# Decode attention, batch by batch through both layers, with part of K and V kept in SBUF, later tiles loaded by half, and K transposed on VectorE

## The chip, the cores and the metric

The kernel runs on one core of one Trainium2 chip. The metric is the device time of one execution, in microseconds, as a median over repeated runs. A run more than 1.5% above the fastest of its kernel counts as slow; only fast runs are compared. PE is the tensor engine, DVE the vector engine, ACT the scalar engine, POOL is GpSimd, and SP is the engine that issues the transfers.

## The reference

Two identical layers are applied to 8 sequences of one token. Each layer is attention over a cache, and then a small MLP, both behind layer norms. Both layers use the *same* caches and the *same* weights. Only the last 1024 of 4096 cache rows are used.

```python
# B=8 batches, D=640, H=32 heads, Dh=128, W=1024 rows of the cache, F=1728
def A(x, k_cache, v_cache, wq, wo):
    q = (x @ wq) split in 32 heads
    k, v = k_cache[:, :, -1024:], v_cache[:, :, -1024:]
    p = softmax(einsum("bhqd,bhkd->bhqk", q, k) * Dh**-0.5)
    return merge_heads(einsum("bhqk,bhkd->bhqd", p, v)) @ wo
def B(x, w1, b1, w2, b2):
    return gelu(layernorm(x) @ w1 + b1) @ w2 + b2
x = x + A(layernorm(x)); x = x + B(layernorm(x))      # layer 0
x = x + A(layernorm(x)); x = x + B(layernorm(x))      # layer 1
```

One head's K or V of one batch is 1024 x 128 bf16, 256 KB. It is called a *tile* below. There are 8 x 32 x 2 = 512 tiles a layer. The kernel before fetches all of them once for each layer: 1024 tiles, 268 MB, and about 25 MB of weights.

Queries and values are so small that attention hardly moves the result. I computed the reference on a CPU twice (values only, beside the timed runs), once as it is and once with `wo` set to zero, so without attention. The largest output is 0.395, the largest difference 0.00195, and the relative difference (2-norm) 0.19%. The kernel before, run for its values alone, differs from the reference by 0.31%. So attention lies below the kernel's own rounding.

## The kernel before

It goes layer by layer, and within a layer batch by batch. For each head, PE transposes K against an identity (8 matmuls of 128 x 128), and DVE or ACT copies the result out of PSUM. Then the transposed K streams as the moving operand of two N=512 matmuls against a query that is masked to one of 32 output rows. P·V has V as stationary operand and one column of P as the moving one, 8 load+matmul pairs a head.

```python
def transpose_head(self, kn, hi):
    kt_ps = psA.tile([P, NC8, P], BF16, tag="kt_ps")
    for c in range(NC8):
        nc.tensor.transpose(kt_ps[:, c, :], kn[:, hi, c, :], ident_bf[:])   # L143
    if evac_ctr[0] % 5 in (1, 3):
        nc.scalar.copy(ktile[:], kt_ps[:])                                   # L145
    else:
        nc.vector.tensor_copy(ktile[:], kt_ps[:])                            # L147
...
def s_matmuls(s_ps, qz, h, ktile):
    for k in range(2):                       # [32 rows, 512 keys] each         L195
        nc.tensor.matmul(s_ps[...512 columns...], lhsT=qz[:, h, :], rhs=ktile[...])
...
def o_matmuls(b, h, vn, hi, ptg):
    for c in range(NC8):                                                       # L238
        nc.tensor.matmul(ot_ps[:, b, h:h + 1], lhsT=vn[:, hi, c, :], rhs=ptg[:, c, h:h + 1], ...)
...
# loads are 1 MB: four heads of K or of V in one transfer, 5 K buffers and 4 V buffers
nc.sync.dma_start(vn[:], A_v_cache[b, h0:h0 + HB, SK - W:, :].rearrange("h (m c) d -> m h c d", c=NC8))
```

The softmax here doesn't subtract the row's maximum and nothing guards it: scores larger than these inputs give would overflow.

Of the kernel before, what the change touches and what calls it, by code (L numbers as in the profile page):

```python
# [9 lines left out]
BF16 = mybir.dt.bfloat16  # L11
ALU = mybir.AluOpType
ACT = mybir.ActivationFunctionType

P = 128
# [13 lines left out]
HB = 4  # L29
K_BUFS = 5  # L30
V_BUFS = 4
KT_BUFS = 10
NPRE = 8
NPRE0 = 8


def kernel(
    tc, A_x, A_k_cache, A_v_cache, A_wq, A_wo, B_x, B_w1, B_b1, B_w2, B_b2, out
):
    return _kernel(tc, A_x, A_k_cache, A_v_cache, A_wq, A_wo, B_x, B_w1, B_b1, B_w2, B_b2, out)  # L40


@with_exitstack
def _kernel(ctx: ExitStack, tc: tile.TileContext, A_x, A_k_cache, A_v_cache, A_wq, A_wo,
# [7 lines left out]
    wpool = ctx.enter_context(tc.tile_pool(name="wpool", bufs=1, side="right"))  # L52
    state = ctx.enter_context(tc.tile_pool(name="state", bufs=1))
    small = ctx.enter_context(tc.tile_pool(name="small", bufs=2))
    kpool = ctx.enter_context(tc.tile_pool(name="kpool", bufs=K_BUFS))
    vpool = ctx.enter_context(tc.tile_pool(name="vpool", bufs=V_BUFS))
    ktpool = ctx.enter_context(tc.tile_pool(name="ktpool", bufs=KT_BUFS))
    ppool = ctx.enter_context(tc.tile_pool(name="ppool", bufs=2))
    qzpool = ctx.enter_context(tc.tile_pool(name="qzpool", bufs=2))
    psA = ctx.enter_context(tc.tile_pool(name="psA", bufs=3, space=bass.MemoryType.PSUM))  # L60

    ident_bf = const.tile([P, P], BF16)
    make_identity(nc, ident_bf[:])
    eps_t = const.tile([P, 1], FP32)
    nc.vector.memset(eps_t[:], EPS)
    mask32 = const.tile([P, H, H], BF16)
    nc.gpsimd.memset(mask32[:], 0.0)
    nc.gpsimd.affine_select(
        out=mask32[:], in_=mask32[:],
        pattern=[[1, H], [-1, H]],  # L70
        compare_op=ALU.not_equal, fill=1.0, base=0, channel_multiplier=0,
    )

    b1_bf = wpool.tile([P, NFC], BF16)
    nc.vector.memset(b1_bf[:], 0.0)
    with nc.allow_non_contiguous_dma(reason="tiny bias load"):
        nc.gpsimd.dma_start(b1_bf[:, 0:13], B_b1[0:13 * P].rearrange("(fc p) -> p fc", p=P))
        nc.gpsimd.dma_start(b1_bf[0:FLAST, 13:14], B_b1[13 * P:F].rearrange("(fc p) -> p fc", p=FLAST))
    b1_f = wpool.tile([P, NFC], FP32)
    nc.vector.tensor_copy(b1_f[:], b1_bf[:])  # L80
    b2_bf = wpool.tile([NB, D], BF16)
    b2_src = bass.AP(tensor=B_b2.tensor, offset=B_b2.offset, ap=[[0, NB], [1, D]])
    nc.gpsimd.dma_start(b2_bf[:], b2_src)
    b2_f = wpool.tile([NB, D], FP32)
    nc.vector.tensor_copy(b2_f[:], b2_bf[:])
    wq_sb = wpool.tile([P, NKC, H * DH], BF16)
    nc.sync.dma_start(wq_sb[:], A_wq.rearrange("(kc p) n -> p kc n", p=P))

    x_bf0 = state.tile([NB, D], BF16)
    nc.sync.dma_start(x_bf0[:], x_in[:, :])  # L90
    x_f = state.tile([NB, D], FP32)
    nc.vector.tensor_copy(x_f[:], x_bf0[:])
    xn_bf = state.tile([NB, D], BF16)
    xnT = state.tile([P, NKC, NB], BF16)
    qT_bf = state.tile([P, H, NB], BF16)
    ot_bf = state.tile([P, NB, H], BF16)
    y_f = state.tile([NB, D], FP32)
    y_bf = state.tile([NB, D], BF16)
    hT_bf = state.tile([P, NFC, NB], BF16)
    zT = state.tile([P, NKC, NB], BF16)  # L100

    def layernorm(src, dst):
        stats = small.tile([NB, 2, 6], FP32, tag="ln_stats")
        nc.vector.bn_stats(stats[:, 0, :], src[:, 0:D // 2])
        nc.vector.bn_stats(stats[:, 1, :], src[:, D // 2:D])
        mv = small.tile([NB, 2], FP32, tag="ln_mv")
        nc.vector.bn_aggr(mv[:], stats[:])  # L107
        rstd = small.tile([NB, 1], FP32, tag="ln_rstd")
        nc.scalar.activation(rstd[:], mv[:, 1:2], ACT.Sqrt, bias=eps_t[:NB, :], scale=1.0)  # L109
        nc.vector.reciprocal(rstd[:], rstd[:])  # L110
        nc.vector.tensor_scalar(out=dst, in0=src, scalar1=mv[:, 0:1], scalar2=rstd[:, 0:1],
                                op0=ALU.subtract, op1=ALU.mult)

    def make_T(ps_pool, src_bf, dst_T):
        pt = ps_pool.tile([P, NKC, NB], BF16, tag="xT_ps")
        for kc in range(NKC):
            nc.tensor.transpose(pt[:, kc, :], src_bf[:, kc * P:(kc + 1) * P], ident_bf[:NB, :NB])
        nc.vector.tensor_copy(dst_T[:], pt[:])

    evac_ctr = [0]  # L120

    class AttnLayer:
        def __init__(self, idx):
            self.idx = idx
            self.pre_kt = {}
            self.k_tiles = {}

        def load_k(self, b, h0, prefetch_only=False):
            key = (b, h0)
            if key in self.k_tiles:  # L130
                return self.k_tiles[key] if prefetch_only else self.k_tiles.pop(key)
            kn = kpool.tile([P, HB, NC8, DH], BF16, tag="kn")
            src = A_k_cache[b, h0:h0 + HB, SK - W:, :].rearrange("h (m c) d -> m h c d", c=NC8)
            nc.sync.dma_start(kn[:], src)
            if prefetch_only:
                self.k_tiles[key] = kn
            return kn

        def transpose_head(self, kn, hi):
            ktile = ktpool.tile([P, NC8, P], BF16, tag="kt")  # L140
            kt_ps = psA.tile([P, NC8, P], BF16, tag="kt_ps")
            for c in range(NC8):
                nc.tensor.transpose(kt_ps[:, c, :], kn[:, hi, c, :], ident_bf[:])  # L143
            if evac_ctr[0] % 5 in (1, 3):
                nc.scalar.copy(ktile[:], kt_ps[:])  # L145
            else:
                nc.vector.tensor_copy(ktile[:], kt_ps[:])  # L147
            evac_ctr[0] += 1
            return ktile

        def prologue_step(self, b, h):
            kn = self.load_k(b, (h // HB) * HB, prefetch_only=True)
            self.pre_kt[(b, h)] = self.transpose_head(kn, h % HB)

        def run(self, mctx, transition_fn=None, pre_q_fn=None, post_o_fn=None):
            li = self.idx

            for h0 in range(0, H, HB)[:5]:
                self.load_k(0, h0, prefetch_only=True)

            if pre_q_fn is not None:
                pre_q_fn()

            with tc.tile_pool(name=f"psq{li}", bufs=1, space=bass.MemoryType.PSUM) as psq:
                layernorm(x_f, xn_bf)
                make_T(psq, xn_bf, xnT)
                qT_ps = psq.tile([P, H, NB], FP32, tag="qT_ps")
                for h in range(H):
                    for kc in range(NKC):
                        nc.tensor.matmul(qT_ps[:, h, :], lhsT=wq_sb[:, kc, h * DH:(h + 1) * DH],  # L170
                                         rhs=xnT[:, kc, :], start=(kc == 0), stop=(kc == NKC - 1))
                nc.vector.tensor_copy(qT_bf[:], qT_ps[:])

            wctx = ExitStack()
            wopool = wctx.enter_context(tc.tile_pool(name=f"wopool{li}", bufs=1, side="right"))
            wo_sb = wopool.tile([P, H, D], BF16, tag="wo")
            nc.sync.dma_start(wo_sb[:], A_wo.rearrange("(h p) n -> p h n", p=P))

            def build_qz(b):
                qz = qzpool.tile([P, H, H], BF16, tag="qz")  # L180
                nc.vector.tensor_tensor(out=qz[:], in0=qT_bf[:, :, b:b + 1].to_broadcast([P, H, H]),  # L181
                                        in1=mask32[:], op=ALU.mult)
                return qz

            with ExitStack() as ictx:
                psS = ictx.enter_context(tc.tile_pool(name=f"psS{li}", bufs=2, space=bass.MemoryType.PSUM))
                psO = ictx.enter_context(tc.tile_pool(name=f"psO{li}", bufs=1, space=bass.MemoryType.PSUM))

                def alloc_s():
                    s_ps = psS.tile([H, NC8, P], FP32, tag="s_ps")  # L190
                    return s_ps

                def s_matmuls(s_ps, qz, h, ktile):
                    for k in range(2):
                        nc.tensor.matmul(s_ps[:, 4 * k:4 * k + 4, :].rearrange("p c m -> p (c m)"),  # L195
                                         lhsT=qz[:, h, :],
                                         rhs=ktile[:, 4 * k:4 * k + 4, :].rearrange("p c m -> p (c m)"),
# [207 lines left out]
```

## Time and profile before

The median is 821.6 us over 6 runs (819.9 to 823.9).

| what | number | where it is read |
|---|---|---|
| traffic | 293 MB, 357 GB/s on average | queue table |
| plateau of the transfers | about 385 GB/s | slices |
| PE busy | 86% | engines |
| chain of waits | 79% PE | chain |
| SP waiting for P·V to free V buffers | 433 us | waits of the DMA queue |

The page's parts for engines, slices (40 slices of the span, DMA in tenths of busy time, GB/s moved), queues and chain:

```profile
span 821.3 us, 21636 instructions
PE 702.5 (86%) x10008; PEld 487.9 (59%) x10008; DVE 263.8 (32%) x449; ACT 236.3 (29%) x285; POOL 7.2 (1%) x15
...
DMA  9999999999999999999899899999999999999814
GB/s 334 375 382 386 386 385 386 386 385 386 383 382 376 386 383 379 382 379 380 311 349 328 320 385 380 369 386 376 382 384 380 386 374 386 377 387 334 300 65 159
...
q1 hardware_dynamic: 148912, 293.05, 97.8%
...
PE 79%; DMA 9%; ACT 6%; DVE 3%; issue 2%; SPq 0%; ACTq 0%; DVEq 0%
```

The costliest groups (line, engine, operation, out<-in with shapes and count | busy us, mean ns of one | idle before, releaser):

```profile
L147 DVE COPY ktile<-kt_ps 128x1024 bf16<-128x1024 bf16 x307 | 205.9, 689 | 397.4 <-PE kt_ps L143 394.5
L145 ACT COPY ktile<-kt_ps 128x1024 bf16<-128x1024 bf16 x205 | 203.9, 1012 | 444.2 <-PE kt_ps L143 434.7
L143 PE MATMUL kt_ps<-ident_bf,kn 128*128 128x128 bf16 x4096 | 288.4, 231 | 33.0 <-DMA kn<-in_A_k_cache_dram 22.8
...
L195 PE MATMUL s_ps<-ktile,qz 128*32 128x512 bf16 x1024 | 272.4, 395 | 1.8 <-DVE qz L181 1.8
...
L238 PE MATMUL po_tile<-ptg,vn 128*128 128x1 bf16 x4096 | 122.3, 164 | 18.1 <-DMA vn<-in_A_v_cache_dram 12.8
```

PE's transposes and scores are 561 of its 702 busy us. At the same time the 16 DMA engines are busy for 97.8% of the span, so the two bounds stand beside each other. The waits of the DMA queue (waiter <- awaited: us in total, times, longest) say that transfers start when P·V frees a buffer:

```profile
SPq L231 <- PE po_tile L238: 433.0, 110, 7.9
```

One line of PE's timeline (start, length, engine, line, operation) is the yardstick for the change's many small matmuls. It shows 160 pairs of weight load and N=8 matmul in 4.41 us, 27.5 ns a pair:

```profile
427.05 4.41 PE L170 MATMUL qT_ps<-xnT,wq_sb 128*128 128x8 bf16 x160 [0.27 <-DVE xnT L118]
```

### The profile page before, as it was taken

How to read it: one execution, taken by the hardware profiler on the slowest of the kernel's cores; microseconds unless marked ns; L12 is line 12 of the kernel's file. 1: busy time of each engine (PE TensorE's matmuls, PEld its weight loads, DVE VectorE, ACT ScalarE, POOL GpSimd, SP SyncE). 2: the span in 40 equal slices, each digit the busy share in tenths (PEclk: the TensorE clock that was granted, in tenths of full speed). 3: DMA queues.
4: the chain of work that ended last, by engine and by line, in shares of the span. 5: the costliest groups of instructions: out<-in, count | busy, mean ns of one | idle time of the engine just before them, and what ended most of it. 6: DMA issues, size and time to landing. Idle time of an engine off the chain costs nothing.

```text
span 821.3 us, 21636 instructions
## 1 busy us (share of the span) xinstructions
PE 702.5 (86%) x10008; PEld 487.9 (59%) x10008; DVE 263.8 (32%) x449; ACT 236.3 (29%) x285; POOL 7.2 (1%) x15
## 2 busy tenths in 40 slices
PE   0889989898989899996759998989898989989463
PEld 0756656566666666666435666666666656666432
DVE  1433332334333332331224433333323333323122
ACT  0234323323233323233003423332232333232200
POOL 2000000000000000000000000000000000000000
PEclk9899989898989989897858998989899998989676
DMA  9999999999999999999899899999999999999814
GB/s 334 375 382 386 386 385 386 386 385 386 383 382 376 386 383 379 382 379 380 311 349 328 320 385 380 369 386 376 382 384 380 386 374 386 377 387 334 300 65 159
DMA packets 149114, 294.44 MB, mean 359 GB/s; under 512 B 4360, under 2 KB 16032, under 8 KB 148384
## 3 DMA queue, kind: packets, MB, share of 16 engines
q1 hardware_dynamic: 148912, 293.05, 97.8%
q8 instruction: 78, 1.28, 0.6%
q0 software_dynamic: 112, 0.01, 0.1%
q14 instruction: 12, 0.10, 0.0%
HBM read 293.04 MB, written 0.01 MB: 357 GB/s over the span
## 4 chain that ended last, share of the span: by engine, by line
PE 79%; DMA 9%; ACT 6%; DVE 3%; issue 2%; SPq 0%; ACTq 0%; DVEq 0%
PE s_ps L195 31%; PE kt_ps L143 29%; PE po_tile L238 13%; ACT ktile L145 4%; DMA kn<-in_A_k_cache_dram 4%; DMA w_sb<-in_B_w_dram 3%; DMA vn<-in_A_v_cache_dram 2%; PE att_ps L301 2%; PE o_ps L347 1%; ACT pe L203 1%; PE qT_ps L170 1%; ACT pe L206 1%; DVE pe L212 1%; PE po_tile L214 1%; PE att_ps L303 1%
## 5 line engine op out<-in xcount | busy, mean ns | idle before, releaser
L147 DVE COPY ktile<-kt_ps 128x1024 bf16<-128x1024 bf16 x307 | 205.9, 689 | 397.4 <-PE kt_ps L143 394.5
L145 ACT COPY ktile<-kt_ps 128x1024 bf16<-128x1024 bf16 x205 | 203.9, 1012 | 444.2 <-PE kt_ps L143 434.7
L143 PE MATMUL kt_ps<-ident_bf,kn 128*128 128x128 bf16 x4096 | 288.4, 231 | 33.0 <-DMA kn<-in_A_k_cache_dram 22.8
L143 PEld LDWEIGHTS <-kn 128*128 128x128 bf16 x4096 | 258.3, 104 | 87.1 <-issue 63.1
L195 PE MATMUL s_ps<-ktile,qz 128*32 128x512 bf16 x1024 | 272.4, 395 | 1.8 <-DVE qz L181 1.8
L238 PEld LDWEIGHTS <-vn 128*128 128x128 bf16 x4096 | 113.4, 97 | 60.4 <-issue 46.6
L195 PEld LDWEIGHTS <-qz 128*32 128x32 bf16 x1024 | 83.8, 98 | 95.0 <-issue 15.7
L238 PE MATMUL po_tile<-ptg,vn 128*128 128x1 bf16 x4096 | 122.3, 164 | 18.1 <-DMA vn<-in_A_v_cache_dram 12.8
L214 PE MATMUL po_tile<-ident_bf,pe 32*128 32x32 bf16 x128 | 5.9, 179 | 32.3 <-DVE pe L212 32.3
L181 DVE TENSOR_TENSOR qz<-qT_bf,mask 128x1024 bf16<-128x1024 bf16 x16 | 19.5, 1224 | 29.9 <-PE s_ps L195 29.7
L214 PEld LDWEIGHTS <-pe 32*128 32x128 bf16 x128 | 4.6, 97 | 39.0 <-ACT pe L206 38.8
L109 ACT ACTIVATE rstd<-mv,eps_t 8x1 f32<-8x1 f32 x6 | 1.8, 293 | 82.8 <-DVE mv L107 82.8
L301 PE MATMUL att_ps<-wo_sb,ot_bf 128*8 128x512 bf16 x64 | 21.7, 441 | 1.0 <-DVE ot_bf L295 1.0
L347 PE MATMUL o_ps<-w_sb,hT_bf 128*8 128x512 bf16 x28 | 11.9, 519 | 9.4 <-DMA w_sb<-in_B_w_dram 9.4
L203 ACT ACTIVATE pe<-s_ps 32x512 bf16<-32x512 f32 x16 | 9.4, 586 | 33.5 <-PE s_ps L195 33.5
L303 PE MATMUL att_ps<-wo_sb,ot_bf 128*8 128x128 bf16 x64 | 15.4, 241 | 0.0
L301 PEld LDWEIGHTS <-ot_bf 128*8 128x8 bf16 x64 | 6.5, 101 | 11.6 <-issue 4.8
L170 PE MATMUL qT_ps<-xnT,wq_sb 128*128 128x8 bf16 x320 | 8.8, 167 | 2.4 <-issue 2.2
L170 PEld LDWEIGHTS <-wq_sb 128*128 128x128 bf16 x320 | 8.7, 101 | 2.5 <-issue 2.5
L206 ACT ACTIVATE pe<-s_ps 32x512 bf16<-32x512 f32 x16 | 9.1, 569 | 0.0
L347 PEld LDWEIGHTS <-hT_bf 128*8 128x8 bf16 x28 | 3.1, 109 | 10.1 <-issue 4.7
L295 DVE CAST ot_bf<-po_tile 128x256 bf16<-128x256 f32 x2 | 0.8, 425 | 24.9 <-PE po_tile L238 24.9
(59 smaller groups left out, 91.0 us busy)
## 6 DMA issues: line engine op xcount, KB each, us to landing
kn<-in_A_k_cache_dram SPq DMA_DIRECT2D x128, 1024.0 KB, 12.2
vn<-in_A_v_cache_dram SPq DMA_DIRECT2D x128, 1024.0 KB, 9.5
wo_sb<-in_A_wo_dram SPq DMA_DIRECT2D x2, 5120.0 KB, 23.1
wq_sb<-in_A_wq_dram SPq DMA_DIRECT2D x1, 5120.0 KB, 16.4
w_sb<-in_B_w_dram SPq DMA_DIRECT2D x2, 2160.0 KB, 7.9
w_sb<-in_B_w_dram SPq DMA_DIRECT2D x2, 2080.0 KB, 14.8
w_sb<-in_B_w_dram SPq DMA_DIRECT2D x2, 80.0 KB, 13.5
x_bf<-in_A_x_dram SPq DMA_DIRECT2D x1, 10.0 KB
```

Of the source, the lines that this page charges most:

```text
L143: nc.tensor.transpose(kt_ps[:, c, :], kn[:, hi, c, :], ident_bf[:])
L145: nc.scalar.copy(ktile[:], kt_ps[:])
L147: nc.vector.tensor_copy(ktile[:], kt_ps[:])
L170: nc.tensor.matmul(qT_ps[:, h, :], lhsT=wq_sb[:, kc, h * DH:(h + 1) * DH], rhs=xnT[:, kc, :], start=(kc == 0), stop=(kc == NKC - 1))
L181: nc.vector.tensor_tensor(out=qz[:], in0=qT_bf[:, :, b:b + 1].to_broadcast([P, H, H]), in1=mask32[:], op=ALU.mult)
L195: nc.tensor.matmul(s_ps[:, 4 * k:4 * k + 4, :].rearrange("p c m -> p (c m)"), lhsT=qz[:, h, :], rhs=ktile[:, 4 * k:4 * k + 4, :].rearrange ...
L203: nc.scalar.activation(pe[:, 0:4, :].rearrange("p c m -> p (c m)"), s_ps[:, 0:4, :].rearrange("p c m -> p (c m)"), ACT.Exp, scale=QSCALE, ...
L214: nc.tensor.transpose(pt_ps[:, c, :], pe[:, c, :], ident_bf[:H, :H])
L238: nc.tensor.matmul(ot_ps[:, b, h:h + 1], lhsT=vn[:, hi, c, :], rhs=ptg[:, c, h:h + 1], start=(c == 0), stop=(c == NC8 - 1))
L301: nc.tensor.matmul(att_ps[:, 0:512], lhsT=lhsT, rhs=wo_sb[:, h, 0:512], start=(h == 0), stop=(h == H - 1))
L303: nc.tensor.matmul(att_ps[:, 512:D], lhsT=lhsT, rhs=wo_sb[:, h, 512:D], start=(h == 0), stop=(h == H - 1))
L347: nc.tensor.matmul(o2_ps[:, 0:512], lhsT=hT_bf[:, fc, :], rhs=w2_sb[:, fc, 0:512], start=(fc == 0), stop=(fc == NFC - 1))
```

## The change

Its intent is to fetch less and to take the K transposes and the wide score matmuls off PE.

1. It is batch-major. Batch b runs through layer 0, its MLP and its queries of layer 1. After layer 0, 14 of its 32 heads keep K and V in SBUF (28 of 41 tile slots), so that layer 1 needs no second fetch of them. The other 18 heads are streamed again. Batch b-1's streamed heads run interleaved with batch b's MLP. Weights are loaded once.
2. DVE transposes K in SBUF, one instruction a tile, as 32-bit words. The code reckons with 32 x 32 blocks, each transposed for itself. So each group of 32 partitions holds *other* keys, and the query is spread into 4 columns, each masked to one group. K becomes the stationary operand (128 keys, stride of two bf16), with 4 moving columns: 8 pairs a head.
3. Heads go in groups of up to 8. Per group: scores, one exp, 16 small PE matmuls that turn P, a copy out of PSUM on DVE, row sums by a matmul with ones, P·V.
4. Loads are one tile each instead of four, from a pool of slots in first-in-first-out order.

The core of the diff (cut):

```diff
-        def transpose_head(self, kn, hi):
-            for c in range(NC8):
-                nc.tensor.transpose(kt_ps[:, c, :], kn[:, hi, c, :], ident_bf[:])
-            ...copy kt_ps -> ktile on DVE or ACT...
+    def load(job, which, h):
+        s = take()
+        n = DH * NC8 // 2 if s in filled else DH * NC8
+        filled.add(s)
+        nc.sync.dma_start(slots[s][:, 0:n],
+                          cache[job.b, h, SK - W:, :].rearrange("(m c) d -> m (c d)", c=NC8)[:, 0:n])
+    def s_head(job, hi):
+        ...
+            nc.vector.transpose(slots[kt] as uint32 "p (j gt c) -> p j gt c",
+                                slots[kn] as uint32 "p (gt j r) -> p j gt r")
+        for g in range(2):
+            for j in range(2):
+                for e in range(2):
+                    o = 512 * j + 256 * g + e
+                    nc.tensor.matmul(job.s_ps[:, hi, g, :], lhsT=k[:, o:o + 255:2],
+                                     rhs=qd[:, h, 2 * j + e, :], ...)
+    def softmax(job):
+        nc.scalar.activation(p_s[:, 0:n], job.s_ps[:, 0:n], ACT.Exp, scale=QSCALE)
+        ...16 matmuls p_s -> p_ps...
+        nc.vector.tensor_copy(job.p_v[:, :, 0:n, :], p_ps[...])
+        ...8 matmuls with ones -> sums...
+    def finish(job):
+        nc.vector.reciprocal(rd[:, 0:n], job.o_ps[:, 1, 0:n])
+        nc.vector.tensor_tensor(out=dst, in0=job.o_ps[:, 0, 0:n], in1=rd[:, 0:n], op=ALU.mult)
+    for b in range(NB):
+        drain(run_jobs(jobs))                          # layer 0 of b, 5 groups
+        ch = chain(b)                                  # MLP and layer-1 query of b
+        merge(run_jobs(again), ch, 1)                  # with layer 1, streamed heads of b-1
+        drain(run_jobs(keep(b, 1)))                    # layer 1, kept heads of b
```

**The line with `n` is not an optimisation that keeps the function.** A slot that has been filled once receives only the first half of its next tile. The other half keeps what lay there before. Nearly all loads (759 of 800) are such halves, so about half of the keys and values that enter attention belong to another head or batch.

## The prediction

> **What bounds the kernel now.** Two things. The page's slices show the DMA engines busy nearly throughout, at about 385 GB/s (queue table: 293 MB, 97.8% of 16 engines' span). The chain of waits is 79% PE: scores 31%, K transposes 29%, P·V 13%. SP spends 433 us waiting for P·V to free V buffers (the DMA queue's waits). Relieving one side alone would gain little.
>
> **What the change does.**
> 1. Traffic. Batch by batch, 14 of 32 heads keep K and V in SBUF between the layers, and weights are loaded once. Cache tiles (256 KB) fetched fall from 1024 to 800. And, unannounced: a slot that was filled once gets only half of its next tile; the other half is stale. About 45 loads are full, 755 are 128 KB. I count 110 MB of cache plus 15 MB of weights: 125 MB, 325 us at 385 GB/s. This is no longer the reference's attention; I expect it to pass only because attention's contribution is tiny here.
> 2. PE. 4096 K transposes (288 us busy) and 1024 N=512 score matmuls (272 us) go. K tiles become stationary, with 4 moving columns: 4096 load+matmul pairs, beside 4096 for P·V as before. Added: about 1920 pairs for softmax, 1280 projection, 2400 per-batch MLP and q. Total about 14,300. The timeline shows 160 such pairs (q, N=8) in 4.41 us at a granted clock of 0.50: 27.5 ns a pair. So PE about 395 us.
> 3. DVE takes the K transposes: 400 instructions of 512 32-bit elements. [...] this trace has no DVE transpose, but its f32 operations fit that (256 elements: 425 ns, 112: 274). Estimate 0.66 to 0.70 us each, 270 us, plus about 80 us of small operations. ACT's 204 us of PSUM copies go.
> 4. DMA issue: 800 loads of one tile instead of 256 of four. An issue on SP's timeline takes 0.37 to 0.51 us: about 330 us.
>
> No engine exceeds 400 us, so dependencies set the time. DVE is in order: the P copy out of PSUM stands before the next group's transposes, so each group of up to 8 heads costs its transposes plus one round of scores, exp, PE transpose and copy; from such hops in the present chain I estimate 1.6 us a group.
>
> **Sum (estimates).** Layer 0 of a batch: 32 x 0.66 + 5 x 1.6 + 3 = 32 us. Layer 1's streamed heads, with MLP and q woven in: 24. Kept heads, PE bound: 10. That is 66 x 8 = 528. The first batch waits for full tiles and all weights (29 MB, 85 us instead of 32): +53. Last stream and tail +38, minus 4 where batch 0 has no stream: about 615; some waits should overlap, so 600 us. All of the gain is on the critical path, since both old bounds fall.
>
> **Signs.** DMA traffic near 125 MB, around 200 GB/s; transposes 0.65 to 0.75 us, x400; PE pairs near 27 ns; DVE idle mostly ended by PE around the softmax copy; a chain mixed between DVE, PE and ACT; a DMA-bound first 85 us.
>
> **What would make it wrong.** Weights read with a stride of two elements may load slower (54 ns a pair would add 110 us to PE). A DVE transpose at half that rate adds 270 us. Too few small loads may be in flight while 28 of 41 slots are kept. If groups overlap better than I think, 500 us. Results could fail the tolerance; the time would stand.
>
> Predicted 600 us, 510 to 690; faster 0.96, same 0.02, slower 0.02.

A straight line through two f32 operations (425 ns for 256 elements, 274 ns for 112) gives 0.69 us for 512 elements, an estimate within the range that was put. The sum came to 615 us, with 0.66 us a transpose, and was rounded to 600 us. That DVE keeps the program's order, and that a stride of two costs no time, is checked below on the trace of the changed kernel (a wait of 1.15 us; 0.21 us a step for both strides).

## The result

The changed kernel takes 637.1 us (635.7 to 638.9, 8 runs), against 822.2 us for the kernel before in 16 runs. The ratio is 0.775 (0.774 to 0.777). Ratios here are the mean time of one kernel's fast runs over that of the other's of the same rounds, so not quite the ratio of the medians that are quoted.

The page after, the same parts:

```profile
span 636.8 us, 31626 instructions
PE 454.4 (71%) x14400; PEld 425.1 (67%) x14400; DVE 325.9 (51%) x855; ACT 20.7 (3%) x99; POOL 13.8 (2%) x27
...
DMA  7999960866768666865677476766677577847620
GB/s 289 388 375 356 310 192 11 234 194 174 200 186 230 171 197 184 237 181 157 181 216 223 138 205 187 226 171 179 175 209 206 160 211 205 234 132 197 188 80 2
...
q1 hardware_dynamic: 122534, 125.22, 66.1%
```

Traffic is 125 MB as counted. After the first five slices the transfers run at about half of their plateau. No engine is busy for more than 71%. The page's chain of waits breaks off in this trace (a stretch of 42 us is given as "issue"), so it isn't used. The groups that replace the five above:

```profile
L239 DVE STREAM_TRANSPOSE slot<-slot 128x512 uint32<-128x512 uint32 x400 | 250.7, 680 | 19.2 <-DMA slot<-in_A_k_cache_dram 14.7
L249 PE MATMUL s_ps<-qd,slot 128*128 128x4 bf16 x4096 | 180.6, 168 | 77.5 <-DVE slot L239 55.2
...
L277 PE MATMUL o_ps<-p_v,slot 128*128 128x1 bf16 x4096 | 169.1, 165 | 19.7 <-DMA slot<-in_A_v_cache_dram 18.4
...
L288 DVE RECIPROCAL rd<-o_ps 128x8 f32<-128x8 f32 (+2 forms) x80 | 15.3, 192 | 115.0 <-PE o_ps L277 114.2
...
L266 DVE CAST p_v<-p_ps 128x64 bf16<-128x64 f32 (+2 forms) x80 | 16.7, 208 | 50.1 <-PE p_ps L262 49.9
```

Scores now wait for DVE's transposes (55 us), and DVE waits 114 us for P·V before it may form a group's result (`finish`, L288) and 50 us before it copies P (L266). SP's waits for P·V have shrunk from 433 us:

```profile
SPq L228 <- PE o_ps L277: 91.0, 102, 19.4
SPq L228 <- DVE slot L239: 62.7, 109, 4.0
```

DVE's timeline of layer 0 of one batch shows the rhythm:

```profile
322.13 4.86 DVE L239 STREAM_TRANSPOSE slot<-slot 128x512 uint32<-128x512 uint32 x8
328.14 0.23 DVE L266 CAST p_v<-p_ps 128x64 bf16<-128x64 f32 x1 [1.15 <-PE p_ps L262]
328.28 4.85 DVE L239 STREAM_TRANSPOSE slot<-slot 128x512 uint32<-128x512 uint32 x8
...
334.28 0.22 DVE L266 CAST p_v<-p_ps 128x64 bf16<-128x64 f32 x1 [0.66 <-PE p_ps L262]
334.43 1.29 DVE L239 STREAM_TRANSPOSE slot<-slot 128x512 uint32<-128x512 uint32 x2
338.26 0.21 DVE L288 RECIPROCAL rd<-o_ps 128x8 f32<-128x8 f32 x1 [2.54 <-PE o_ps L277]
...
338.64 0.17 DVE L266 CAST p_v<-p_ps 128x16 bf16<-128x16 f32 x1
338.73 4.85 DVE L239 STREAM_TRANSPOSE slot<-slot 128x512 uint32<-128x512 uint32 x8
```

Eight transposes take 4.85 us, 0.61 us each. From the end of a group's transposes to the start of the next group's, DVE loses 1.3 us (326.99 to 328.28) where the group has 8 heads, and 3.0 us (335.72 to 338.73) behind the group of 2, where PE still has eight heads of P·V and projection to do. DVE keeps the program's order here: the copy waits 1.15 us for PE, and the eight transposes that the program has behind it start only after the copy has, at 328.28. With the copy on ACT and `finish` later, ten transposes run across such a group's end without a pause (act_copy_defer below, 6.04 us).

The three stages of one batch in the steady state, by windows of the trace (busy us and instructions of each engine, granted clock, DMA share, GB/s): the streamed heads of the batch before with this batch's MLP and query (from DVE's addition of attention to x up to the first score of a kept head); the kept heads (up to the first transpose of the next batch); layer 0 of the next batch.

```profile
285.85:313.21 27.36, 20.91 (x673) 20.19 (x674) 15.35 (x46) 0.82 (x5) 1.08 (x2) 1.00 0.62 173
313.21:322.13 8.92, 7.45 (x278) 7.32 (x274) 1.33 (x9) 0.43 (x2) 0.00 (x0) 1.00 0.51 158
322.13:355.62 33.49, 25.98 (x796) 23.57 (x796) 23.04 (x50) 1.06 (x5) 0.00 (x0) 1.00 0.75 215
```

The columns in parentheses belong to PE, PE's weight loads, DVE, ACT and POOL in this order. In no stage is any engine, or the DMA, busy all the time.

A mark in the trace tells batches apart: DVE adds each batch's attention to its x once. These marks stand at 88.3, 147.5, then on average every 69.6 us up to 565.4 us, and the rest takes 71.4 us. The six middle batches are the *steady period* below, each between two marks.

### The profile page after: what moved, and what is told of

Same layout as the page of the kernel before. It is cut to its first block, busy times and chain, and to the rows that moved or that the text cites. A ratio compares the mean times of both kernels' runs of the same rounds, so it can differ in the third digit from the quotient of the medians.

```text
span 636.8 us, 31626 instructions
## 1 busy us (share of the span) xinstructions
PE 454.4 (71%) x14400; PEld 425.1 (67%) x14400; DVE 325.9 (51%) x855; ACT 20.7 (3%) x99; POOL 13.8 (2%) x27
## 3 DMA queue, kind: packets, MB, share of 16 engines
q1 hardware_dynamic: 122534, 125.22, 66.1%
## 5 line engine op out<-in xcount | busy, mean ns | idle before, releaser
L239 DVE STREAM_TRANSPOSE slot<-slot 128x512 uint32<-128x512 uint32 x400 | 250.7, 680 | 19.2 <-DMA slot<-in_A_k_cache_dram 14.7
L249 PE MATMUL s_ps<-qd,slot 128*128 128x4 bf16 x4096 | 180.6, 168 | 77.5 <-DVE slot L239 55.2
L249 PEld LDWEIGHTS <-slot 128*128 128x128 bf16 x4096 | 146.4, 105 | 103.2 <-DVE slot L239 71.9
L277 PE MATMUL o_ps<-p_v,slot 128*128 128x1 bf16 x4096 | 169.1, 165 | 19.7 <-DMA slot<-in_A_v_cache_dram 18.4
L277 PEld LDWEIGHTS <-slot 128*128 128x128 bf16 x4096 | 144.2, 104 | 21.2 <-DMA slot<-in_A_v_cache_dram 19.6
L288 DVE RECIPROCAL rd<-o_ps 128x8 f32<-128x8 f32 (+2 forms) x80 | 15.3, 192 | 115.0 <-PE o_ps L277 114.2
L305 PE MATMUL att<-ot,wo_sb 128*128 128x1 bf16 x1280 | 62.1, 165 | 2.4 <-issue 1.8
L305 PEld LDWEIGHTS <-wo_sb 128*128 128x128 bf16 x1280 | 49.8, 104 | 2.8 <-issue 1.8
L270 PE MATMUL o_ps<-p_v,ones_bf 128*128 128x8 bf16 (+2 forms) x640 | 28.3, 167 | 29.2 <-DVE p_v L266 29.2
L270 PEld LDWEIGHTS <-ones_bf 128*128 128x128 bf16 x640 | 29.5, 104 | 28.7 <-issue 26.7
L266 DVE CAST p_v<-p_ps 128x64 bf16<-128x64 f32 (+2 forms) x80 | 16.7, 208 | 50.1 <-PE p_ps L262 49.9
L388 PE MATMUL q_ps<-xn,wq_sb 128*128 128x1 bf16 x1280 | 38.5, 165 | 2.1 <-DVE xn L166 1.7
L183 PEld LDWEIGHTS <-w_sb 128*128 128x128 bf16 x630 | 18.6, 104 | 4.7 <-DVE yT L171 2.9
L205 PEld LDWEIGHTS <-w_sb 128*128 128x128 bf16 x630 | 18.6, 104 | 3.5 <-DVE g L199 2.0
```

Source lines behind the costliest of these rows:

```text
L183: nc.tensor.matmul(h_ps[:, fc, :], lhsT=w1_sb[:, kc, fc * P:(fc + 1) * P], rhs=yT[:, kc, :], start=(kc == 0), stop=(kc == NKC - 1))
L205: nc.tensor.matmul(o_ps[:, n, :], lhsT=w2_sb[:, fc, n * P:(n + 1) * P], rhs=g2[:, fc, :], start=(fc == 0), stop=(fc == NFC - 1))
L239: nc.vector.transpose(slots[kt][:].bitcast(U32).rearrange("p (j gt c) -> p j gt c", j=2, c=32), slots[kn][:].bitcast(U32).rearrange("p (gt ...
L249: nc.tensor.matmul(job.s_ps[:, hi, g, :], lhsT=k[:, o:o + 255:2], rhs=qd[:, h, 2 * j + e, :], start=(j == 0 and e == 0), stop=(j == 1 and ...
L266: nc.vector.tensor_copy(job.p_v[:, :, 0:n, :], p_ps[:, :, 0:2 * n].rearrange("p t (h g) -> p t h g", g=2))
L270: nc.tensor.matmul(job.o_ps[:, 1, 0:n], lhsT=ones_bf[:], rhs=job.p_v[:, c % 4, 0:n, c // 4], start=(c == 0), stop=(c == NC8 - 1))
```

## The experiments

All twelve kernels of the experiments were accepted as correct, which says little about attention, as will be seen. The first four ran on one chip and the next two sets of four on others, each set with its own runs of the kernel before (822.9, 820.9 and 825.7 us).

| kernel | loads | us | ratio to before | first mark, us | steady period, us |
|---|---|---|---|---|---|
| changed | halves, 14 kept | 637.1 | 0.775 | 88.3 | 69.6 |
| full_loads | whole, 14 kept | 697.8 | 0.848 | 92.0 | 77.1 |
| nokeep_half | halves, 0 kept | 671.1 | 0.816 | 89.3 | 73.7 |
| nokeep_full | whole, 0 kept | 778.3 | 0.947 | 92.5 | 87.4 |
| no_reload | once per slot | 616.1 | 0.749 | 72.3 | 68.6 |
| act_copy | halves, 14 kept | 625.6 | 0.761 | 88.3 | 68.3 |
| act_copy_defer | halves, 14 kept | 622.9 | 0.758 | 88.7 | 67.8 |
| skew | halves, 14 kept | 626.3 | 0.762 | 89.6 | 68.4 |
| skew_full | whole, 14 kept | 701.3 | 0.855 | 92.0 | 77.8 |
| skew_no_reload | once per slot | 599.9 | 0.728 | 76.6 | 66.1 |
| skew_keep8 | halves, 8 kept | 628.0 | 0.762 | 88.6 | 68.0 |
| fused | halves, 14 kept | 625.3 (3 fast runs) | 0.757 | not used | not used |
| fused_full | whole, 14 kept | 702.0 | 0.852 | 92.4 | 77.7 |

### Where the gain comes from: undoing the halves and the keeping

**full_loads** loads every tile whole, and so computes the reference:

```diff
-        n = DH * NC8 // 2 if s in filled else DH * NC8
+        n = DH * NC8
```

> Every cache tile loaded whole, so this one computes the reference's attention. Cache 800 x 256 KB = 210 MB, with weights about 225 MB. Theory A (in the changed kernel the DMA is off the critical path by a small margin, DVE/PE dependencies set its 69 us a batch): 26.2 MB a batch is 68 us at 385 GB/s against 69 us, and the 9.7 us with only kept heads have few free slots to fill, so some of it comes out on top: 680 to 720 us, DMA busy over 90%. Rival B (halved loads are a main source of the gain and the whole kernel is still paced by its data): about 637 x 225/125, over 800 us, no gain left over the kernel before.

Measured: 697.8 us (695.9 to 698.7), inside theory A's range. The queue table and the transposes' group of this run:

```profile
q1 hardware_dynamic: 122534, 224.70, 91.0%
...
L239 DVE STREAM_TRANSPOSE slot<-slot 128x512 uint32<-128x512 uint32 x400 | 254.8, 684 | 39.8 <-DMA slot<-in_A_k_cache_dram 35.8
```

With whole tiles the DMA is again nearly the bound (91% busy), and DVE's transposes wait 36 us for K instead of 15 us. So with 14 heads kept the halving is worth 61 us of the 185 us, and the function-keeping rest of the change gains 15%.

**nokeep_half** sets `NKEEP = 0` and leaves the halves in.

> NKEEP = 0, half loads left in. 112 more K tiles are loaded and transposed (DVE +68 us busy, DMA +29 MB). Theory A (time is the sum of stages whose length DVE's order and PE set; kept heads only shift the K transposes out of a PE-bound stage of 9.7 us): the kept stage vanishes and the streamed layer-1 stage grows by 14 x 0.6 us + one group: 625 to 655 us, about the same as with kept heads. Rival B (keeping heads is what gained, by traffic or by transposes): 637 + 40 to 70 us.

Measured: 671.1 us (668.1 to 674.6), between the two: keeping heads is worth 34 us here, not the 0 to 18 us of A nor the 40 to 70 us of B. DVE has 512 transposes instead of 400, and they wait 42 us for K instead of 15 us, so both DVE and the supply of K have less room. Theory A had put the whole effect down to the order of stages and is too simple.

**nokeep_full** does both.

> NKEEP = 0 and full loads: 1024 full tiles, 283 MB, so nearly the kernel before's traffic with the new PE and DVE work. Theory A: DMA bound, 283 MB at 385 GB/s = 735 us, measured 740 to 775 us; so the new way of computing alone, at equal cache traffic, gains 50 to 80 us by filling the DMA's gaps. Rival B (the way of computing gains nothing without less data): 810 to 830 us.

Measured: 778.3 us (776.7 to 783.5), just above theory A's range. The queue table:

```profile
q1 hardware_dynamic: 154790, 283.44, 100.0%
```

At nearly the traffic of the kernel before (283 against 293 MB), the new way of computing gains 44 us and leaves the DMA busy for the whole span. The gain then can only be what a steadier stream and 10 MB fewer weights (an estimate of 25 us at 385 GB/s) give. Batch-major order, transposes on DVE and small loads weren't undone one by one, so their shares of the 44 us stay open.

The parts one after the other, whole tiles first: 822 → 778 (new computing) → 698 (14 heads kept, 59 MB less) → 637 us (halves, 99 MB less). At the plateau of 385 GB/s these two cuts are 152 us and 258 us of transfer time. They brought 81 and 61 us. The difference is where the transfers ceased to be the bound. With the halves first the same end is reached by 778 → 671 → 637 us: then the halves bring 107 us and the kept heads 34 us. So neither part has a share of its own; what each is worth depends on whether the other is there.

**no_reload** fills each slot once and never again:

```diff
-        n = DH * NC8 // 2 if s in filled else DH * NC8
+        if s not in filled:
+            nc.sync.dma_start(...the whole tile...)
         filled.add(s)
-        nc.sync.dma_start(...n columns...)
```

> Wrong on purpose: a slot is loaded once and never again, later heads read whatever lies there. Only about 26 MB move after which the DMA is idle. Theory A (half loads are off the critical path after the first batch): only the first batch gets shorter, by 6 to 10 us: 620 to 632 us. Rival B (loads, or SP issuing 800 of them, still pace the steady state): below 600 us. On the result: if the comparison with the reference passes here too, the tolerance can not see attention, and passing says nothing about the half loads.

Measured: 616.1 us (615.9 to 616.6), a little below A's range and far from B's. Of the 21 us, 16 us lie before the first mark (88.3 to 72.3 us), where the first batch waits for whole tiles and weights. A steady period falls from 69.6 to 68.6 us. So in the changed kernel the transfers cost 1 us a batch once it is under way: theory A, though the first batch gained more than the 6 to 10 us that I had expected. And a kernel whose attention runs almost wholly on stale data passes. The comparison with the reference can't see attention with these inputs.

To see the fault of the halves itself I ran three programs for their values on a CPU, with both caches multiplied by 400, which makes attention up to 0.38 of an output of at most 0.63. The relative errors (2-norm) against the reference with the same inputs are 0.0056 for the kernel before, 0.0056 for full_loads and 0.585 for the changed kernel. These runs give values only, no times.

### What sets the steady period: DVE's order, PE's order, or the tiles

The prediction said that DVE's order makes each group cost one softmax round on top of its transposes. Three kernels take parts of that round away step by step.

**act_copy** lets ACT copy P:

```diff
-        nc.vector.tensor_copy(job.p_v[:, :, 0:n, :], p_ps[...])
+        nc.scalar.copy(job.p_v[:, :, 0:n, :], p_ps[...])
```

> The changed kernel with the copy of P out of PSUM moved from DVE to ACT (half loads left in). Theory A (DVE's order is what each group pays: its transposes of the next group stand behind this copy, 1.3 us from the last transpose of a group to the first of the next in the trace): DVE passes the softmax, but still waits in finish for the last P.V of the group before; about 0.5 us on each of 64 transposing groups saved: 600 to 618 us. Rival B (PE's own stream sets the pace: it waits for exp and copy whichever engine copies): 632 to 642 us.

Measured: 625.6 us (622.2 to 628.6). That is neither A's 600 to 618 nor B's 632 to 642.

**act_copy_defer** also calls `finish` two heads into the next group:

```diff
             for hi in range(GH):
+                if hi == 2 and fin is not None:
+                    finish(fin); old, fin = (fin if fin.layer == 0 else None), None
                 ...
-            if prev is not None:
-                finish(prev)
+            old, fin = None, prev
```

> As the last, and finish (reciprocal and product on DVE) put two heads later, behind the first two transposes of the next group, so that DVE has nothing to wait for between groups. Theory A: transposes run on through the softmax, 585 to 612 us, the pause between groups gone from DVE's timeline. Rival B: 630 to 642 us.

Measured: 622.9 us (619.9 to 626.1), again between the two. Theory A's sign did come: the pause between two groups of 8 is gone where nothing else holds DVE. This is DVE's timeline of layer 0 of one batch:

```profile
318.60 6.04 DVE L239 STREAM_TRANSPOSE slot<-slot 128x512 uint32<-128x512 uint32 x10
325.75 4.87 DVE L239 STREAM_TRANSPOSE slot<-slot 128x512 uint32<-128x512 uint32 x8 [1.10 <-PE s_ps L249]
...
330.82 0.70 DVE L239 STREAM_TRANSPOSE slot<-slot 128x512 uint32<-128x512 uint32 x1
331.71 0.71 DVE L239 STREAM_TRANSPOSE slot<-slot 128x512 uint32<-128x512 uint32 x1 [0.19 <-PE s_ps L249]
334.35 0.21 DVE L288 RECIPROCAL rd<-o_ps 128x8 f32<-128x8 f32 x1 [1.93 <-PE o_ps L277]
```

Ten transposes now run in one go across the group's end. But then DVE stands still for 1.1 us because a slot to write to is still being read by scores on PE, and for 1.9 us because P·V is not done. The wait wasn't removed but moved. The sum shows it too: in the changed kernel DVE waits 50 us in all before the copy of P, and 14 us came, while the wait before `finish` grew from 114 to 138 us.

**skew** changes PE's order as well, so that PE has scores of the next group to do while ACT forms exp and copies P:

```diff
+                    s_head(job, hi)
+                    if hi == len(job.heads) - 1:
+                        sm_exp(job)                  # exp right after the group's last score
+                if prev is not None and hi == 0:
+                    sm_turn(prev)                    # PE turns P one head into the next group
+                if prev is not None and hi == LAG - 1:
+                    sm_sum(prev)                     # LAG = 2
+                ...o_head(prev, hi - LAG), finish and projection later still...
```

> As the last, and PE's order changed too: a group's exp is issued right after its last score, and its PE transpose, sums and P.V come one and two heads into the next group, so that PE has scores to do meanwhile. If both engines pay for the softmax round (theory C: DVE's stall and PE's stall of 0.35 us at two places of each of 80 groups are hidden in each other, and only removing both shows): 555 to 590 us, and the difference to the last is 20 us or more. If DVE alone paid (A): within 10 us of the last.

Measured: 626.3 us (623.9 to 628.0), no better than the last. Theory C's number falls: freeing PE of the softmax round, too, brings nothing. But this order also puts P·V later, and `finish` still stands on DVE, before transposes:

```profile
L295 DVE RECIPROCAL rd<-o_ps 128x8 f32<-128x8 f32 (+2 forms) x80 | 15.5, 194 | 161.4 <-PE o_ps L284 161.4
```

The copy's 50 us of waiting are gone from DVE, and the wait before `finish` is 47 us longer than in the changed kernel: 161 us for both then (50 + 114 = 164 us in the changed kernel), in both kernels partly where DVE has nothing else to do. So no run had a DVE that doesn't wait for PE between groups, and theory C was not tested in full.

**skew_no_reload** asks whether the supply of tiles had taken the stall's place: it is skew with the edit of no_reload.

> Wrong on purpose: the reordered kernel (P copied by ACT, finish late, PE skewed) with slots loaded once and never again, as in the run that only took the loads away (616 us). Theory D (the two waits stand in parallel: with the softmax stall removed the steady state falls back on the supply of tiles, as loads wait for one of the 13 slots that the kept heads leave, which ate the gain): taking both away gives much more than the sum of the two single gains (21 us and 11 us): 560 to 590 us. Rival E (after the stall something else on PE or DVE, not supply, keeps the 69 us a batch): 600 to 612 us, about the sum of the single gains.

Measured: 599.9 us (599.3 to 600.4), at the lower edge of E's range. Rival E stands and theory D falls: taking away the transfers (21 us) and the stalls (11 us) brings 37 us together, only 5 us above the sum. The same three stages as above, in this run:

```profile
265.83:292.77 26.94, 20.76 (x678) 19.88 (x679) 15.03 (x43) 1.63 (x8) 1.08 (x2) 1.00 0.01 3
292.77:301.37 8.60, 7.64 (x273) 7.26 (x269) 1.11 (x7) 0.84 (x4) 0.00 (x0) 1.00 0.01 4
301.37:332.88 31.51, 25.30 (x796) 22.73 (x796) 22.00 (x46) 2.07 (x10) 0.00 (x0) 1.00 0.02 4
```

With no reloads to wait for and no copy of P in DVE's order, layer 0 is 31.5 us instead of 33.5 us, and the first stage has hardly moved (26.9 against 27.4 us). PE is busy for 54 us of 67 us, DVE for 38 us. So taking the round's copy and the transfers away together is worth 3.5 us of a period of 69.6 us. The other 66 us lie elsewhere. That is not the worth of all of DVE's waits for PE: within layer 0 its pauses between transposes fell only from 6.9 to 4.4 us, since `finish` waits for P·V before the transposes that follow it, once for 2.5 us. There the chain of waits of this run goes through `finish`, from P·V to the transposes of the next group (start, length, what):

```profile
316.98 0.23 PE o_ps L284 x8
317.23 0.22 DVE rd L295
317.48 0.17 DVE ot L301
317.64 4.77 DVE slot L240 x8
```

No run took `finish` off DVE.

Where the other 66 us lie is argued, not shown. It is probably PE's stream of small pairs, and the fill and drain of three stages in turn: 14,400 pairs over the whole kernel, at the 26.7 ns a pair of PE's timeline, are 384 us, and of PE's idle time within a period (13 us of 67 us here) 9 us are scores that wait for DVE's transposes (53.3 us in six periods). No run took pairs away from PE, so how much they bind stays open. It is also open how much a PE that waits less in one place loses in the next because DVE's transposes are then late; the waits of scores for transposes rose from 55 to 85 us between the changed kernel and skew:

```profile
PE s_ps L250 <- DVE slot L240: 84.8, 144, 8.0
```

The chain of waits of skew_no_reload, which covers nearly all of its span, shows the same mixture, with shares of the span by engine:

```profile
PE 50%; DVE 22%; issue 13%; DMA 10%; POOL 2%; SPq 1%; ACT 1%; POOLq 0%; ACTq 0%
```

### For speed: other splits, and the versions that compute the reference

**skew_keep8** keeps 8 heads, so that 12 more slots are free for the stream.

> The reordered kernel with half loads and 8 kept heads instead of 14: 12 more slots for the stream, 48 more K tiles to load and transpose (DVE +30 us busy, DMA +12.6 MB). Theory D: the slots gained are worth more than the transposes cost: 595 to 618 us. Rival E: slower than with 14 kept, 630 to 645 us, as without kept heads in the original order (671 for 0 kept).

Measured: 628.0 us (627.0 to 630.0), the same as with 14 within the runs' scatter (626.3). It falls between the ranges of D and E: the added transposes and transfers and the freed slots seem to cancel (argued from the total alone). Between 8 and 14 the time is flat; with 0 kept the original order lost 34 us.

**fused** puts the kept heads' groups into one run of groups with the next batch's layer 0:

```diff
-            jobs = nxt + kept
+            jobs = keep(b - 1, 1) + nxt + kept
-        drain(run_jobs(keep(b, 1)))
```

> The reordered kernel with half loads, 14 kept heads, and the kept heads' second-layer groups put into the same run of groups as the next batch's first layer, so that DVE can transpose while PE works on kept heads and their slots come free during the stream. Theory D: slots come free no earlier in PE's order, but one pipeline drain a batch is saved, 2 to 3 us each: 600 to 615 us. Rival E: the same 2 to 3 us, so this run is for speed, not for telling apart.

Measured: 625.3 us in the three fast runs (620.3 to 626.6), outside the expected 600 to 615. The fourth, the profiled one, was slow (630.8 us), so its trace is not used. The saving of a drain (2 to 3 us a batch, the estimate) is not to be seen.

**skew_full** and **fused_full** are skew and fused with whole tiles, the candidates for a fast kernel that computes the reference.

> The last with full loads, so that it computes the reference's attention. 225 MB at 385 GB/s are 584 us; the first batch and the tail have about 25 us with little DMA. With the compute side relieved, DMA should be the bound: 640 to 675 us, DMA busy over 92%, against 698 us with full loads alone.

> The same with full loads, computing the reference's attention. The DMA is nearly the bound (91% busy in 698 us with full loads alone), so only its gaps can be won: 670 to 695 us.

Measured: 701.3 us (698.3 to 705.4) and 702.0 us (699.0 to 704.5). Both missed their ranges; neither is faster than full_loads alone (697.8 us). The waits of skew_full say where the freed time went:

```profile
DVE slot L240 <- DMA slot<-in_A_k_cache_dram: 87.8, 86, 7.8
```

DVE waits 88 us for K tiles, against 36 us in full_loads, with the DMA 90.5% busy. With whole tiles the transfers are the bound, and a better order of computing only waits longer for them.

So no run beat the changed kernel while computing the reference. The kernel to use of those measured is full_loads: 15% faster than before, and right.

## Why the prediction was right or wrong

The time was 637 us against 600 us predicted, within 510 to 690 us, and the gain was clear. Point by point:

- **Traffic, 125 MB: right** (125.2 MB), with the halves seen beforehand. That the result would pass because attention is tiny was right, and no_reload and the CPU values show it.
- **PE, 14,300 pairs of 27.5 ns: right.** There are 14,400. PE's timeline where scores and P·V alternate, in steps of 8 pairs:

```profile
316.48 0.35 PE L249 MATMUL s_ps<-qd,slot 128*128 128x4 bf16 x8
316.69 0.35 PE L277 MATMUL o_ps<-p_v,slot 128*128 128x1 bf16 x8
...
318.19 0.35 PE L249 MATMUL s_ps<-qd,slot 128*128 128x4 bf16 x8
```

  The starts of the first and the last line are 64 pairs and 1.71 us apart, 26.7 ns a pair. The 0.35 us of a step is longer than the 0.21 us to the next because one matmul's record lasts 165 ns (L277's mean): seven starts of 26.7 ns and one record are 0.35 us. The fear of slow loads with a stride of two was unfounded. One load's record is 104 ns here, but loads overlap and a pair starts every 26.7 ns. Stride 2 (scores) is no slower than stride 1 (P·V): 0.21 us a row of eight for both.
- **Transposes, 0.66 to 0.70 us: right for one, slightly high for a row of them.** One is 0.68 us in the profile, and eight take 4.85 us, 0.61 us each.
- **No engine exceeds 400 us: wrong for PE**, whose busy time is 454 us, since every short row of pairs ends with a record of 165 ns that is counted as busy in full. It didn't matter for the sum, which was built from pairs.
- **The sum, 615 us: nearly right, stage by stage.** The first mark was put at 85 us and came at 88.3. Batch 0's second part (66 - 4 = 62 us) took 59.2. Six periods of 66 us took 69.6 each. The end (24 + 10 + 38 = 72 us) took 71.4. So the miss is 3.6 us in each of six periods, 22 us. It sits in two terms: the stage of streamed heads with MLP and query (24 us, measured 27.4; the kept heads, 10 us, took 8.9) and layer 0 (32 us, measured 33.5, with a drain of 7 us behind the last transposes where 3 us and one round, 4.6 us, were put, and 3.0 us behind the group of two).
- **"Some waits should overlap, so 600 us": wrong.** This step had no number behind it. The measured time lies above the sum, not below it, and the step made the prediction worse by 15 us.
- **"The P copy stands before the next group's transposes, so each group costs its transposes plus one round, 1.6 us": right as a description, overstated as a cost.** The pause is there (1.3 us). But taking the copy out of DVE's order brought 11 to 14 us of the 50 us that DVE waits before it, and the wait before `finish` grew by 24 to 47 us in the same runs. The sign "DVE idle mostly ended by PE around the softmax copy" had it too: DVE's larger wait was the 114 us before `finish`, for P·V, which the prediction doesn't name. A stall that comes back at the engine's next need of PE was counted as if it were the price. What the waits before `finish` cost in all is not shown.
- **All of the gain is on the critical path since both bounds fall: right in direction**, but the bounds didn't fall equally. With the transfers at 283 MB, only 44 us came, and each further cut of the traffic brought less than its transfer time.
- **First 85 us bound by the DMA: right.** no_reload shortened it by 16 us, and it is the only place where the changed kernel's transfers cost much.

## What to carry to other kernels

Undo a large change one part at a time before its gain is explained, and check first that each part keeps the function: here the last third of the gain (61 of 185 us, with the other parts in place) came from loads that leave half of each tile stale, and a comparison in which attention is below rounding couldn't see it. A pause on one engine's timeline is not worth its length (here, of 50 us of waits before the copy 11 to 14 us were won): before it is removed, look for the next thing that the engine needs from the other, since the wait can come back there. In a sum of stages, leave out rounding for "overlap" that has no number.

## Costs measured here

- A DVE transpose of 128 x 512 uint32 takes 680 ns (the mean of 400 in the changed kernel), and 0.61 us each in a row of eight. Viewed as bf16 that is 128 x 1024.
- A pair of a full weight load (128 x 128) and a matmul of 1 to 8 columns takes 26.7 to 27.5 ns: 27.5 ns at a granted clock of 0.50 (q in the kernel before, 8 columns), and 26.7 ns where the trace gives 1.00 (scores and P·V in the changed kernel, 4 and 1 columns).
- The DMA engines' busy time per MB is 3.37 us in nokeep_half, mostly 1 KB pieces (77.7% of 669.7 us for 154.6 MB), and 2.74 us in nokeep_full, 2 KB pieces (100.0% of 777.0 us for 283.4 MB): 23% more. In the first of these the DMA wasn't saturated, so how much of the 23% is due to the size of the pieces wasn't shown.
